# Pacing the loads of the first-layer weight pieces in SyncE's queue

## The chip, the core and the metric

The kernel runs on one core of one Trainium2 chip. A core has five engines that run side by side: TensorE (PE in the profile, its weight loads PEld), VectorE (DVE), ScalarE (ACT), GpSimd (POOL) and SyncE (SP). Here SyncE does nothing but issue DMA transfers, one after the other in the order of the program; ScalarE issues a few at the start and the end. The metric is the time of one execution on the device in microseconds (us). Three executions of the kernel before took 669.35, 664.38 and 667.37 us; the median is 667.37.

## The reference

Two blocks follow one another. The first is a delta-rule attention over 768 steps for 4 x 8 heads of size 48; the second is a layer pair with a learned negative slope on 3072 tokens.

```python
k_n = k / (np.linalg.norm(k, axis=-1, keepdims=True) + 1e-06)
for t in range(S):                                   # S = 768
    y[:, :, t] = np.einsum('bhd,bhde->bhe', q[:, :, t], state)
    v_old = np.einsum('bhde,bhd->bhe', state, kt)
    state = state + bt[:, :, :, None] * np.einsum('bhd,bhe->bhde', kt, vt - v_old)

x = y as (B*S, H*D) = (3072, 384)
h = x @ w_in                                         # (384, 2048)
g = np.maximum(h, 0.0) + alpha * np.minimum(h, 0.0)
out = g @ w_out                                      # (2048, 384)
```

`w_in` and `w_out` arrive as 8-byte floats; everything is computed in 4-byte floats.

## The kernel before, in words

The 768 steps are cut into 12 chunks of 64, and the 4 batches into 2 pairs, so that there are 24 attention steps `n`, each for one chunk and one pair. Inside a chunk the recurrence becomes small matrix products and the inverse of a triangular matrix, which VectorE makes by elimination for four steps at a time (`eliminate_small` for the first four, `eliminate` after that). When both pairs of a chunk are done, its 256 tokens go through the two layers. The order of every engine's instructions is written out by hand, and products of the layers are woven between those of the attention (`weave`, `alongside`).

**The weight pieces.** `w_in` is cut into 12 pieces of 128 rows by 512 columns; as 8-byte floats a piece is 512 KB. `weights` (L183) returns three things for such a list: `fetch` (L206) issues the loads on SyncE's queue, up to a given piece; `begin` (L220) has ScalarE turn the two 32-bit words of each number into parts of a 4-byte float (two instructions a piece, L226 and L227); `finish` (L232) has VectorE join them (L237, L242). A piece is first loaded into a stage, which is space that nothing else needs yet: pieces 0 to 5 lie in the later home of `w_out`, 6 and 7 in `space_out`, 8 and 9 in `more`, 10 in `sums`, and piece 11 again in the first stage. A second call of `weights` does the same for the 16 pieces of `w_out`.

**Where the loads stand in SyncE's queue.** Calls and lines are in this order: the first loads of `k`, `beta`, `q`, `v` (L137, L161, L174, L1584); `fetch_in(n_in)` and `fetch_in(n_in + 2)`, that is pieces 0 to 7 in a row (L1585, L1644, `n_in` is 6); `load_late(1)` and `load_v(2)`, that is four loads of `kl` and two of `v_raw` (L1646, L1647); three `load_early`, six loads of `ke` for steps 4, 5 and 6 (L1656); `fetch_in(n_in + 5)`, pieces 8 to 10 (L1657); `load_q(2)` and `load_q(3)`, four loads of `qp` (L1662); after the first chunk one `load_early` (L1525), `load_late(2)` (L1706), `fetch_in(n_in + 6)`, which is piece 11 (L1709), `load_late(3)` and `load_v(3)` (L1713, L1714), and so on.

**Who uses them.** ScalarE begins pieces 0 to 2 at L1671 and pieces 3 and 4 at L1674, right before it places the first inverses (`place_small`, L631, called from `first_chunk`); pieces 0 to 3 are joined inside `first_chunk`, the rest beside the second chunk (`second_pair`). The key blocks of steps 4, 5 and 6 are turned on TensorE in `first_chunk` (`flipped`, L404); the queries of steps 2 and 3 are turned at L1710 (`flips`, L404).

**Completion semaphores.** In the built program the DMA transfers take eight completion semaphores in turn, and a transfer is issued only when the one that used its semaphore before, eight transfers earlier, has landed.

Of the kernel before, what the change touches and what calls it, by code (L numbers as in the profile page):

```python
# [26 lines left out]
U32 = mybir.dt.uint32  # L27
# [16 lines left out]
def kernel(  # L44
# [11 lines left out]
    nc = tc.nc  # L56
# [13 lines left out]
    const = ctx.enter_context(tc.tile_pool(name="const", bufs=1))  # L70
# [109 lines left out]

    ahead = [0]

    def weights(pieces, stages, ids, done, limit=None, pool=False):  # L183

        count = len(pieces)
        fetched, begun = [], []

        def words(i):
            w = stages[ids[i]]
            dst, src = pieces[i]
            shape = list(dst.shape)
            n = shape[1] * (shape[2] if len(shape) > 2 else 1)  # L200
            w = w[:, 0 : 2 * n]
            if len(shape) > 2:
                return w.rearrange("p (f e) -> p f e", f=shape[1]), n
            return w, n

        def fetch(n):  # L206
            while len(fetched) < min(n, count):
                i = len(fetched)
                assert ids[i] not in ids[len(done) : i]
                nc.sync.dma_start(out=words(i)[0], in_=pieces[i][1].bitcast(U32))  # L210
                fetched.append(i)

        def flat(x):
            return x.rearrange("p f d -> p (f d)") if len(x.shape) > 2 else x

        def halves(i):
            w = flat(words(i)[0]).rearrange("p (e w) -> p e w", w=2)
            return w[:, :, 0], w[:, :, 1], flat(pieces[i][0])

        def begin(n):  # L220
            while len(begun) < min(n, count):
                i = len(begun)
                assert i < len(fetched)
                lo, hi, dst = halves(i)

                nc.scalar.activation(dst.bitcast(U32), lo, ACT.Copy, scale=2.0**-29)  # L226
                nc.scalar.activation(  # L227
                    lo.bitcast(FP32), hi.bitcast(FP32), ACT.Prelu, scale=2.0**-112, alpha=-(2.0**32)
                )
                begun.append(i)  # L230

        def finish():  # L232
            for i in range(count):
                begin(min(i + 2, max(ahead[0], i + 1)))
                lo, _, dst = halves(i)
                engine = nc.gpsimd if pool else nc.vector
                engine.tensor_scalar(  # L237
                    out=lo, in0=lo, scalar1=3, scalar2=None, op0=ALU.logical_shift_left
                )
                yield  # L240

                engine.tensor_tensor(  # L242
                    out=dst.bitcast(U32), in0=lo, in1=dst.bitcast(U32), op=ALU.add
                )
                done.append(i)
                n = len(fetched)
                while n < min(count, limit or count) and ids[n] not in ids[i + 1 : n]:
                    n += 1
                    fetch(n)
                yield  # L250

        return fetch, begin, finish()


# [12 lines left out]
    for t in range(2):  # L267
# [5 lines left out]
        out=ones, in_=ones, compare_op=ALU.is_ge, fill=1.0, base=0,  # L273
# [7 lines left out]
    for t in range(2):  # L281
# [5 lines left out]
        out=first_of, in_=ident.rearrange("p (q u e) -> p u q e", u=2, e=HB // 2)[:, 0],  # L287
# [7 lines left out]
        out=below[:, 0:1], in0=below[:, 0:1], scalar1=-1.0, scalar2=1.0, op0=ALU.mult, op1=ALU.add  # L295
    )
    nc.gpsimd.tensor_tensor(
        out=below[:, 1:2], in0=which[:, 1:2], in1=below[:, 1:2], op=ALU.subtract
# [1045 lines left out]
    in_done, out_done = [], []  # L1344
# [185 lines left out]
    def statics(first, last):  # L1530
# [18 lines left out]
    pieces = [  # L1549
        (w_in[:, i, o : o + W_IN_P], moe_w_in[i * 128 : (i + 1) * 128, o : o + W_IN_P])  # L1550
        for o in range(0, DFF, W_IN_P)
        for i in range(KT)
    ]
    n = 2 * W_IN_P
    n_in = FT * DM // n
    stages = [space[:, i * n : (i + 1) * n] for i in range(n_in)]
    spare_words = space_out.rearrange("p s e -> p (s e)")
    stages += [spare_words[:, i * n : (i + 1) * n] for i in range(2)]
    words = more.rearrange("p i s e -> p (i s e)").bitcast(U32)
    stages += [words[:, i * n : (i + 1) * n] for i in range(2)]  # L1560
    stages += [sums.rearrange("p i s e -> p (i s e)").bitcast(U32)[:, 2 * n : 3 * n]]
    ids = [*range(n_in + 5), 0]
    fetch_in, begin_in, conv_in = weights(pieces, stages, ids, in_done, n_in + 5)
    PARTS_IN = 2 * len(pieces)

    pieces = [(w_out[:, f], moe_w_out[f * 128 : (f + 1) * 128]) for f in range(FT)]
    stages = [space_out[:, i] for i in range(SPACES)]
    for f in range(FT // 2, FT, 2):
        stages.append(w_out[:, f : f + 2].rearrange("p f d -> p (f d)").bitcast(U32))
    ids = [0, 1, 2, 3, 4, 5, 6, 0, 1, 2, 6, 0, 1, 2, 0, 1]  # L1570
    fetch_out, _, conv_out = weights(pieces, stages, ids, out_done)
    PARTS_OUT = 2 * len(pieces)

# [362 lines left out]
```

## Time and profile before

| | |
|---|---|
| median of three runs | 667.37 us (664.38 to 669.35) |
| the profiled execution | 668.62 us, its span 666.9 us |
| PE busy | 640.3 us (96% of the span) |
| DVE busy | 490.6 us (74%) |
| ACT busy | 266.4 us (40%) |
| POOL busy | 94.8 us (14%) |
| moved by DMA | 37.69 MB, mean 57 GB/s |
| mean granted TensorE clock | 0.984 |

The span runs from the first to the last instruction; the execution is 1.7 us longer. The page cuts the span into 40 slices of 16.7 us and gives each engine's busy share in tenths, so that one sees where an engine is full. The chain of work that ended last starts at the last instruction and goes back, at each step, to what released it. SyncE's instructions are DMA issues: their start and duration say how long the queue was held, and the time to landing runs from the start of the issue until the data has arrived.

### The profile page before, as it was taken

How to read it: one execution, taken by the hardware profiler on the slowest of the kernel's cores; microseconds unless marked ns; L12 is line 12 of the kernel's file. 1: busy time of each engine (PE TensorE's matmuls, PEld its weight loads, DVE VectorE, ACT ScalarE, POOL GpSimd, SP SyncE). 2: the span in 40 equal slices, each digit the busy share in tenths (PEclk: the TensorE clock that was granted, in tenths of full speed). 3: DMA queues.
4: the chain of work that ended last, by engine and by line, in shares of the span. 5: the costliest groups of instructions: out<-in, count | busy, mean ns of one | idle time of the engine just before them, and what ended most of it. 6: DMA issues, size and time to landing. Idle time of an engine off the chain costs nothing.

```text
span 666.9 us, 21587 instructions
## 1 busy us (share of the span) xinstructions
PE 640.3 (96%) x9279; PEld 567.4 (85%) x9279; DVE 490.6 (74%) x1175; ACT 266.4 (40%) x619; POOL 94.8 (14%) x210
## 2 busy tenths in 40 slices
PE   5778799999999999999999999999999999999997
PEld 4576687756688998998998998998999999999997
DVE  4846679996899869748959748859869658568283
ACT  5835656525455343334334333223234245042140
POOL 7000021101010100001000000000035034053260
PEclk9969999999999999999999999999999999999999
DMA  7965545401342032022022022022112210100000
GB/s 117 287 144 117 179 106 126 104 18 32 65 94 40 17 67 49 15 61 49 15 48 38 15 48 37 14 49 37 27 37 38 36 37 4 25 14 1 25 1 25
DMA packets 111152, 37.69 MB, mean 57 GB/s; under 512 B 104224, under 2 KB 107440, under 8 KB 111056
## 3 DMA queue, kind: packets, MB, share of 16 engines
q1 hardware_dynamic: 109184, 35.81, 24.1%
q8 instruction: 73, 1.20, 0.7%
q10 hardware_dynamic: 1872, 0.49, 0.4%
q14 instruction: 23, 0.19, 0.1%
HBM read 31.56 MB, written 4.72 MB: 54 GB/s over the span
## 4 chain that ended last, share of the span: by engine, by line
PE 83%; DVE 9%; ACT 3%; issue 2%; DMA 1%; SPq 1%; POOL 0%; DVEq 0%; POOLq 0%; ACTq 0%
PE p_ffn L991 21%; PE p_ffn L1056 17%; PE p_more L1308 8%; PE p_ffn L1034 5%; PE p_more L1224 4%; PE p_ffn L1214 3%; PE p_ffn L1308 3%; PE p_ffn L1219 2%; PE p_pair L673 2%; PE p_pair L404 2%; PE p_pair L733 2%; PE p_pair L849 2%; PE p_pair L456 2%; PE p_pair L776 2%; PE p_pair L836 2%
## 5 line engine op out<-in xcount | busy, mean ns | idle before, releaser
L991 PE MATMUL p_ffn<-xt,w_in 128*128 128x256 f32 x768 | 177.5, 384 | 3.0 <-ACT w_out L226 1.2
L991 PEld LDWEIGHTS p_ffn<-xt,w_in 128*128 128x128 f32 x768 | 142.6, 190 | 24.5 <-issue 2.2
L1001 ACT ACTIVATE act<-p_ffn 128x512 f32<-128x512 f32 x56 | 33.3, 595 | 80.8 <-PE p_ffn L991 80.5
L1003 DVE SCALAR_TENSOR_TENSOR act<-act,al_t,p_ffn 128x256 f32<-128x256 f32 x112 | 48.5, 474 | 22.7 <-ACT act L1001 22.6
L561 DVE TENSOR_TENSOR block<-block,prod 128x30 f32<-128x30 f32 (+9 forms) x150 | 49.8, 332 | 5.2
L1248 POOL TENSOR_TENSOR k_t<-k_t 128x128 f32<-128x128 f32 (+1 forms) x48 | 29.6, 616 | 166.4 <-ACT k_t L1243 163.9
L555 DVE TENSOR_TENSOR prod<-block 128x30 f32<-128x30 f32 (+9 forms) x150 | 48.9, 326 | 1.4
L1056 PE MATMUL p_ffn<-w_out,act 128*128 128x192 f32 x288 | 49.6, 328 | 0.0
L393 POOL TENSOR_TENSOR beta_t<-beta_t,rec 128x8 f32<-128x8 f32 x24 | 6.2, 258 | 299.5 <-DVE rec L387 287.7
L896 ACT COPY xt<-p_pair 128x384 f32<-128x384 f32 x22 | 10.4, 479 | 91.2 <-PE p_pair L888 77.4
L1056 PEld LDWEIGHTS p_ffn<-w_out,act 128*128 128x128 f32 x288 | 46.5, 190 | 0.3
L1248 POOL TENSOR_TENSOR block<-block 128x128 f32<-128x128 f32 (+1 forms) x48 | 28.0, 583 | 16.7 <-ACT block L1243 14.1
L1214 PE MATMUL p_ffn<-xt,w_in 128*128 128x256 f32 x96 | 28.7, 380 | 0.0
L743 DVE TENSOR_TENSOR r<-v_raw,p_pair 64x192 f32<-64x192 f32 (+1 forms) x66 | 23.3, 352 | 2.2 <-PE p_pair L733 1.2
L685 ACT COPY inv<-p_pair 32x256 f32<-32x256 f32 x40 | 14.5, 361 | 24.9 <-DVE u L840 24.2
L725 ACT COPY y<-p_pair 128x384 f32<-128x384 f32 x22 | 10.4, 480 | 32.3 <-PE p_pair L721 30.7
L1076 DVE TENSOR_TENSOR o_sb<-u,p_ffn 128x192 f32<-128x192 f32 x24 | 8.0, 352 | 20.4 <-PE p_ffn L1056 20.0
L1262 DVE SCALAR_TENSOR_TENSOR act<-block,al_t,act 128x256 f32<-128x256 f32 x32 | 19.1, 638 | 5.1 <-ACT block L1258 5.1
L1308 PE MATMUL p_more<-w_out,act 128*128 128x192 f32 x128 | 21.9, 329 | 0.0
L1243 ACT COPY k_t<-p_more 128x512 f32<-128x512 f32 x16 | 9.4, 586 | 30.6 <-PE p_more L1224 25.9
L1034 PE MATMUL p_ffn<-w_out,act 128*128 128x384 f32 x64 | 21.5, 489 | 0.0
L733 PE MATMUL p_pair<-beside,k_t 48*64 48x112 f32 x704 | 21.3, 259 | 0.2 <-ACT beside L432 0.2
(275 smaller groups left out, 1408.2 us busy)
## 6 DMA issues: line engine op xcount, KB each, us to landing
qp<-in_q_dram SPq DMA_DIRECT2D x48, 96.0 KB, 3.0
v_raw<-in_v_dram SPq DMA_DIRECT2D x48, 96.0 KB, 2.9
kl<-in_k_dram SPq DMA_DIRECT2D x96, 48.0 KB, 2.6
out_dram<-o_sb SPq DMA_DIRECT2D x90, 48.0 KB, 1.6
space_out<-in_moe_w_out_dram SPq DMA_DIRECT2D x11, 384.0 KB, 3.5
ke<-in_k_dram SPq DMA_DIRECT2D x43, 96.0 KB, 3.1
w_out<-in_moe_w_in_dram SPq DMA_DIRECT2D x7, 512.0 KB, 5.8
w_out<-in_moe_w_out_dram SPq DMA_DIRECT2D x5, 384.0 KB, 7.0
```

Source lines behind the costliest of these rows:

```text
L555: nc.vector.tensor_tensor(out=prod, in0=r[:, 0:j, j : j + 1].to_broadcast([128, j, n]), in1=r[:, j : j + 1, j + 1 : HB].to_broadcast([128, ...
L561: nc.vector.tensor_tensor(out=r[:, 0:j, j + 1 : HB], in0=r[:, 0:j, j + 1 : HB], in1=prod, op=ALU.add)
L733: nc.tensor.matmul(p[half(t ^ a), a, g], k_t[n][dims(a), g, half(t)], beside[bp][dims(a), t, g])
L991: nc.tensor.matmul(p_h[:, i], w_in[:, t, (f + i) * 128 : (f + i + 1) * 128], xt[:, t], start=(t == 0), stop=(t == KT - 1),)
L1001: nc.scalar.activation(g, p_h, ACT.Relu, scale=-1.0)
L1003: nc.vector.scalar_tensor_tensor(out=g[:, i], in0=g[:, i], scalar=al_t[:, f + i : f + i + 1], in1=p_h[:, i], op0=ALU.mult, op1=ALU.add,)
L1034: nc.tensor.matmul(p_o[u], gs[f // 2][:, f % 2, u * 128 : (u + 1) * 128], w_out[:, f], start=(f == 0), stop=(f == FT - 1),)
L1056: nc.tensor.matmul(p, x(i), w(i), start=(i == 0), stop=(i == FP - 1))
L1214: nc.tensor.matmul(p[:, f * 256 : f * 256 + 256], w(2, f), xt[:, 2], start=True, stop=False)
L1224: nc.tensor.matmul(q[:, j], a, b, start=True, stop=True)
L1248: nc.gpsimd.tensor_tensor(out=dst, in0=a, in1=b, op=ALU.add)
L1308: nc.tensor.matmul(p, x(i), w(i), start=(i == 0), stop=(i == FP - 1))
```

## The change

`weights` takes a further argument `apart`, which only the call for `w_in` sets, to 2. Before piece `i` is issued, `paced` puts a DMA copy of 4 bytes into SyncE's queue: it reads one word of the stage of piece `i - 2` (for piece 11, of piece 10) and writes it to a new small tile `held_back`, which nothing reads. As the copy reads what the earlier piece's load writes, SyncE waits for that landing before it issues the copy, and what stands behind it in the queue waits too. Pieces 0 and 1 have no such copy; pieces 2 to 11 do, so ten copies are added. In the built program all other instructions of SyncE and those of the other engines keep their order.

```diff
+    holds, held_back = [], const.tile([1, 16], U32, name="held_back")
+
-    def weights(pieces, stages, ids, done, limit=None, pool=False):
+    def weights(pieces, stages, ids, done, limit=None, pool=False, apart=None):
...
+        def paced(i, apart):
+
+            if i >= apart:
+                before = words(i - apart)[0]
+                before = before if len(before.shape) == 2 else before[:, 0]
+                nc.sync.dma_start(out=held_back[0:1, len(holds) : len(holds) + 1], in_=before[0:1, 1:2])
+                holds.append(i)
+
         def fetch(n):
             while len(fetched) < min(n, count):
                 i = len(fetched)
                 assert ids[i] not in ids[len(done) : i]
+                if apart:
+                    paced(i, apart if i < 11 else 1)
                 nc.sync.dma_start(out=words(i)[0], in_=pieces[i][1].bitcast(U32))
                 fetched.append(i)
...
-    fetch_in, begin_in, conv_in = weights(pieces, stages, ids, in_done, n_in + 5)
+    fetch_in, begin_in, conv_in = weights(pieces, stages, ids, in_done, n_in + 5, False, 2)
```

## The prediction

> **What bounds the kernel now.** I read the page's slices and its chain first, then the chain from 27 to 64 us, then SyncE's and ScalarE's timelines there, and last the DMA issues piece by piece.
>
> ```profile
> PE   5778799999999999999999999999999999999997
> ...
> PE 83%; DVE 9%; ACT 3%; issue 2%; DMA 1%; SPq 1%; POOL 0%; DVEq 0%; POOLq 0%; ACTq 0%
> ```
>
> From the seventh slice (100 us) on, TensorE is full; there the change moves nothing. All pieces are loaded in the first 60 us, where TensorE is 50 to 80% busy and the chain goes from engine to engine. A microsecond won or lost there goes through to the end, unless it falls into a wait that something else sets. The chain there:
>
> ```profile
> 29.58 0.36 DVE inv L627
> 29.94 0.14 issue
> 30.07 2.45 PE p_pair L776 x103
> 32.52 1.37 issue
> 33.89 2.62 PE p_pair L776 x70
> ...
> 55.60 0.60 SPq L161
> ...
> 58.32 0.60 SPq L137
> 58.92 0.05 issue
> 58.97 3.65 DMA v_raw<-in_v_dram
> ```
>
> Two places matter: the inverse at 29 to 37 us, beside which ScalarE converts pieces, and 50 to 62 us, where SyncE's queue itself is on the chain: loads stand one behind the other until `v_raw` of step 3 lands, for which VectorE sat idle 4.42 us.
>
> SyncE's queue around the pieces (start, us, issues):
>
> ```profile
> 15.39 3.28 SPq L210 DMA_DIRECT2D w_out<-in_moe_w_in_dram  x6
> 18.79 0.90 SPq L210 DMA_DIRECT2D space_out<-in_moe_w_in_dram  x2
> 19.79 4.21 SPq L161 DMA_DIRECT2D kl<-in_k_dram  x4
> 24.89 1.87 SPq L137 DMA_DIRECT2D v_raw<-in_v_dram  x2
> 27.99 7.00 SPq L137 DMA_DIRECT2D ke<-in_k_dram  x6
> 35.03 2.09 SPq L210 DMA_DIRECT2D more<-in_moe_w_in_dram  x2
> ```
>
> Eight pieces leave in 4.3 us and then drain: from 18 to 27 us the DMA moved 399 GB/s, one piece per 1.3 us. Asked for single issues, the DMA view gives for piece 0 and piece 4:
>
> ```profile
> w_out<-in_moe_w_in_dram SPq DMA_DIRECT2D x1, 512.0 KB, 4.2
> w_out<-in_moe_w_in_dram SPq DMA_DIRECT2D x1, 512.0 KB, 7.3
> ```
>
> So 4.2 us with nothing large ahead, and more with each piece ahead (piece 1: 4.9). Pieces 0 and 1 land at 19.5 and 20.8 us, piece 4 at 24.9, piece 7 at 30.3.
>
> **The change, part by part.** *The copies' own cost.* The trace has no 4-byte copy. The nearest rows of SyncE are a piece's issue, 0.43 us, and the issue of a small table (`al_sb`, 8 KB), 0.60 us. I take 0.45 with the 0.05 us between issues, so 0.5 a copy (bounds 0.4 and 0.65). Nobody waits for a copy to land.
>
> *Pieces 2 to 7.* Each round of two is one landing (4.2 us) plus a copy's issue (0.5): 4.7 us where before a round took 2.6. Piece 2 is issued at 20.0 and lands at 24.2; piece 4 lands at 19.5 + 2 x 4.7 = 28.9; piece 6 at 33.6, piece 7 at 20.8 + 3 x 4.7 = 34.9 (issued at 30.6). ScalarE asks for piece 2 at 24.75, piece 3 at 26.62 (lands at 25.5) and piece 4 at 27.90:
>
> ```profile
> 27.90 0.68 ACT L226 ACTIVATE w_in<-w_out 128x512 uint32<-128x512 uint32 x1
> 28.62 0.68 ACT L227 ACTIVATE w_out<-w_out 128x512 f32<-128x512 f32 x1
> 29.31 0.91 ACT L631 ACTIVATE inv<-inverse,which 128x256 f32<-128x256 f32 x2
> 31.38 0.59 ACT L795 COPY act<-p_pair 128x512 f32<-128x512 f32 x1 [1.16 <-PE p_pair L776]
> ```
>
> Only piece 4 is late, by 1.0 us. Behind it on ScalarE wait the inverse of step 1 (L631), which TensorE needs at 31.87, and the copy L795, before which ScalarE sat idle 1.16 us. So up to 1.16 us costs nothing; I take 0. With piece 1's 4.9 us and 0.65 a copy, piece 4 lands at 30.6, 2.7 late, and costs 1.6. Earlier than now it can't bring anything: ScalarE waited for no piece there.
>
> *What queues behind piece 7.* Four `kl` and two `v_raw` start at 31.1 instead of 19.8, at 0.65 us each; the keys of step 4 are issued at 35.0 and 35.7 and land by 39.9 (4.2 us is the slowest of the six `ke` landings now, 3.1 the quickest). TensorE turns them at 40.86: covered, by 1 us. One of these six issues held the queue for 2.01 us instead of 0.63; one such stall ahead would make it 0.4 us late. Steps 5 and 6 are turned at 47.18 and 49.36, far later. `kl` and `v_raw` of this group are used at 52.47 and 57.73.
>
> *Pieces 8 to 10 and the queries.* The six `ke` end at 39.0, pieces 8 and 9 with their copies at 40.9. The copy for piece 10 waits for piece 8: issued at 39.5, landing 5.3 us later as now, at 44.8. Piece 10 leaves at 45.3, then four `qp` until 48.4 instead of 40.9. They land in 5.4 to 7.0 us now, behind three pieces, so the first two by 52 behind one; they are turned at 53.09. SyncE is next needed at 50.38, which leaves 2 us. ScalarE begins pieces 8 to 10 at 60.95 or later. Cost 0.
>
> *Piece 11.* Its copy (piece 10 landed long before) stands between `load_late(2)` and piece 11, in the stretch where the queue is on the chain. Behind it wait piece 11, four `kl` and the two `v_raw`. This 0.5 us nothing hides: `v_raw` lands that much later, and VectorE and TensorE behind it (TensorE idle for 2.23 us until 65.51).
>
> *Sum.* 0.5 (bounds 0.4 and 0.65) + 0 (to 1.6) + 0 (to 0.4) = +0.5 us, upper bound 2.65. The profiled execution of 668.62 would take 669.1; it lies 1.25 above the median of the runs, so against the median I forecast **667.9**. The runs shown spread by 5 us, and 1% (6.7 us) is about what a measurement of this kernel can tell from no change.
>
> The Trainium skill, "DMA: Bandwidth & Descriptors", section "Anatomy of one DMA", gives about 2.0 us fixed plus bytes by 436 GB/s, fitted for GpSimd's path; as an estimate that is 3.2 us for a piece, against 4.2 in this trace. By it a round would take 3.7 us, piece 4 would land at 26.9, and the sum would stay at +0.5. The rule speaks against pacing all the same: two pieces in flight leave the fixed part uncovered.
>
> **Rivals.** *1. Two in flight land as slowly as five did (slower).* Place: ScalarE's wait for piece 4. It decides from a landing of 4.3 us on (19.5 + 2 x 4.8 = 29.1, where the 1.16 us are used up), and each further microsecond costs two. At piece 4's present 7.3 us: 19.5 + 2 x 7.8 = 35.1, 7.2 late, less 1.16, plus 0.5: +6.5, and 674. For it: the threshold is near, and small `k` packets share the queue. Against it: landings grew with the number ahead, and here at most one is ahead. At 4.9 us a piece and 0.65 a copy the price is 2.2, 669.6.
>
> *2. TensorE's stalls without a wait go (faster).* Between 15 and 70 us two "issue" gaps of 1.37 and 1.50 us stand before L776; the instruction queue fetched 16 KB during each (start 31.16 and 41.64), and one took 1.37 us, another 0.88. Fewer pieces in flight could serve them sooner. At most 2.87 - 0.5 = 2.4 us less: 665.0. Against it: after each fetch 1.4 to 1.5 us passed before TensorE went on, and pieces are in flight at both times after the change too. The Trainium skill, "DMA: Bandwidth & Descriptors", section "Queues, rings and completion order", says that each DMA engine turns between queues packet by packet; by that rule the weights never held a fetch long, and the sum stays at +0.5.
>
> *3. The granted clock falls elsewhere.* Windows (length, PE busy and count, PEld, DVE, ACT, POOL, clock, DMA):
>
> ```profile
> 32.00:37.00 5.00, 3.11 (x103) 2.76 (x96) 1.16 (x2) 1.17 (x2) 0.00 (x0) 0.50 0.51 95
> 37.00:47.50 10.50, 8.20 (x262) 7.51 (x263) 5.24 (x11) 3.65 (x8) 0.00 (x0) 0.66 0.75 191
> 47.50:53.00 5.50, 5.50 (x82) 4.68 (x80) 4.23 (x12) 3.81 (x8) 0.00 (x0) 0.64 0.12 22
> 53.00:60.00 7.00, 6.88 (x162) 5.91 (x155) 4.58 (x10) 4.01 (x8) 0.00 (x0) 1.00 0.69 151
> ```
>
> The clock drops to 0.50 after TensorE's idle 2.5 us at 27.5. If idle times move and it stays up from 37 to 53, the 13.7 us of matmuls shrink by up to 4.8, with rival 2 to 660.2; if it drops from 53 to 60, up to 6.9 are added, to 674.8. The Trainium skill, "TensorE: Matmul & The Clock Gate", Part 1, says that activity is judged in free-running windows of 3.4 us; by that, which way it goes is chance from run to run.
>
> *4. The change doesn't pace.* If the copies don't hold the pieces, only their issues stay: piece 7 and what follows 3 us later with ample cover, and 0.5 at piece 11: 667.9 again.
>
> **From this to the numbers.** Forecast 0.54. Rival 1: 0.16, half of it near 670 and half beyond 1%. Rival 2: 0.12. Rival 3: 0.14, of it 0.05 slower by over 1%, 0.06 faster by over 1%, 0.03 within. Rival 4: 0.04. Faster by over 1% is then 0.06 and a rounding, 0.07; slower 0.08 + 0.05 = 0.13; within 0.80. The range leaves out rival 1's far half and rival 3's ends (0.19): from 665.0 less 1 to 670 plus 2 for the spread of the medians, 664 to 672.
>
> **What would show it.** Right: SyncE's issues of pieces 2 to 7 in pairs some 4.7 us apart, landings near 4.2 us, GB/s from 18 to 32 us nearer 225 than 399; ScalarE idle about 1 us before piece 4 (now L239), L795 still released by TensorE; turning the keys of step 4 not waiting for a DMA; about 0.5 us more before `v_raw` of step 3. Wrong: landings of 5 us and more with an idle ScalarE ahead of L631's successor, a DMA as releaser of L404, the two "issue" gaps gone, or half clock in other stretches.

## The result and the profile after

| | before | after |
|---|---|---|
| median of nine runs each, same chip | 667.73 us (664.38 to 669.36) | 671.47 us (669.59 to 672.08) |
| profiled execution | 668.62 us | 670.56 us |
| its span | 666.9 us | 668.8 us |
| mean granted TensorE clock | 0.984 | 0.987 |

The ratio is 1.0052, with a 95% interval from 1.0032 to 1.0071: the changed kernel takes about 3.5 us longer (2.1 to 4.7). That lies within 1%, the forecast's likeliest case, and inside its range, but it is clear of zero, and the sum in the prediction was 0.5 us.

The page of the changed kernel first: the row of TensorE and of its clock in 40 slices, and the shares of the chain.

```profile
PE   5777799999999999999999999999999999999997
...
PEclk9978799999999999999999999999999999999999
...
PE 80%; DVE 12%; DMA 2%; issue 2%; ACT 2%; SPq 1%; POOL 0%; DVEq 0%; POOLq 0%
```

The row of TensorE differs from the one before in the fourth slice alone (7 for 8, 50 to 67 us), and from the sixth slice on it is full again. What TensorE lost on the chain (83% to 80%) went to VectorE (9% to 12%) and to waits for DMA (1% to 2%). So the place to look at is the one the prediction named, the first 60 us. SyncE's queue in the changed kernel there (start, us, issues):

```profile
20.06 0.62 SPq L214 DMA_DIRECT2D held_back<-w_out  x1
20.72 0.38 SPq L223 DMA_DIRECT2D w_out<-in_moe_w_in_dram  x1
23.52 0.58 SPq L214 DMA_DIRECT2D held_back<-w_out  x1
24.15 0.38 SPq L223 DMA_DIRECT2D w_out<-in_moe_w_in_dram  x1
...
30.32 0.38 SPq L223 DMA_DIRECT2D space_out<-in_moe_w_in_dram  x1
30.81 2.72 SPq L161 DMA_DIRECT2D kl<-in_k_dram  x4
33.57 2.38 SPq L137 DMA_DIRECT2D v_raw<-in_v_dram  x2
36.00 4.84 SPq L137 DMA_DIRECT2D ke<-in_k_dram  x6
...
45.81 0.58 SPq L214 DMA_DIRECT2D held_back<-more  x1
46.44 0.38 SPq L223 DMA_DIRECT2D sums<-in_moe_w_in_dram  x1
46.92 2.77 SPq L137 DMA_DIRECT2D qp<-in_q_dram  x4
49.80 1.55 SPq L137 DMA_DIRECT2D ke<-in_k_dram  x2
51.45 3.57 SPq L161 DMA_DIRECT2D kl<-in_k_dram  x4
55.06 0.64 SPq L214 DMA_DIRECT2D held_back<-sums  x1
55.80 0.34 SPq L223 DMA_DIRECT2D w_out<-in_moe_w_in_dram  x1
56.67 2.70 SPq L161 DMA_DIRECT2D kl<-in_k_dram  x4
59.46 1.27 SPq L137 DMA_DIRECT2D v_raw<-in_v_dram  x2
```

The copies hold the queue (L214, each 0.57 to 0.73 us), pieces 2 to 7 leave in pairs, and everything behind moves: the queries leave from 46.92 on instead of 37.70. At 49.80 the loads for step 7 (`ke`, one call of `load_early`) follow with no pause; before, the queue stood idle from 40.9 until 50.38 at this place:

```profile
37.70 3.21 SPq L137 DMA_DIRECT2D qp<-in_q_dram  x4
50.38 1.75 SPq L137 DMA_DIRECT2D ke<-in_k_dram  x2
```

The last line of the changed kernel's queue is the issue of `v_raw` of step 3, 59.46 instead of 58.32.

TensorE's longest waits from 15 to 70 us in the changed kernel (waits by what ended them: total, times, longest):

```profile
PE p_pair L789 <- issue: 4.4, 2, 4.0
PE p_pair L417 <- DVE w_out L250: 1.6, 1, 1.6
...
PE p_pair L417 <- DMA qp<-in_q_dram: 1.1, 1, 1.1
```

Two of these are new: TensorE now waits for queries before it turns them (L417; the wait of 1.6 us put down to VectorE ends as the last query lands, at 54.46). The first line was 2.9, 2, 1.5 before. The chain shows the same two places:

```profile
30.49 1.81 PE p_pair L789 x104
32.31 3.98 issue
36.28 1.62 PE p_pair L789 x79
...
40.03 0.40 issue
...
47.66 4.59 DMA qp<-in_q_dram
...
52.38 0.64 PE p_pair L417 x4
...
60.11 3.58 DMA v_raw<-in_v_dram
```

The stall without a wait behind the first inverse is 3.98 us for 1.37, the second 0.40 for 1.50. The queries' load, which was on no chain before, is on it, and behind it come loads again, up to `v_raw` of step 3. VectorE takes that at 63.78 instead of 62.71 us.

From there to the end it takes 605.1 us after and 604.2 before; so of the 1.9 us between these two executions 1.1 arise ahead of this moment and 0.9 behind it. In all 14 profiles of this study (before, after and the twelve experiments) this rest lies between 604.2 and 605.1 us, while the moment itself lies anywhere from 60.3 to 66.4. Most of the difference between kernels is made ahead of it.

### The profile page after: what moved, and what is told of

It is laid out like the page before. It is cut to its first block, busy times and chain, and to the rows that moved or that the text cites. A ratio compares the mean times of both kernels' runs of the same rounds, so it can differ in the third digit from the quotient of the medians.

```text
span 668.8 us, 21603 instructions
## 1 busy us (share of the span) xinstructions
PE 640.3 (96%) x9279; PEld 565.9 (85%) x9279; DVE 491.5 (73%) x1175; ACT 266.1 (40%) x619; POOL 94.2 (14%) x210
## 4 chain that ended last, share of the span: by engine, by line
PE 80%; DVE 12%; DMA 2%; issue 2%; ACT 2%; SPq 1%; POOL 0%; DVEq 0%; POOLq 0%
PE p_ffn L1004 19%; PE p_ffn L1069 17%; PE p_more L1321 8%; PE p_ffn L1047 5%; PE p_more L1237 4%; PE p_ffn L1227 3%; PE p_ffn L1321 3%; PE p_ffn L1232 2%; PE p_pair L789 2%; PE p_pair L417 2%; PE p_pair L862 2%; PE p_pair L686 2%; PE p_pair L746 2%; PE p_pair L469 2%; PE p_pair L849 2%
## 5 line engine op out<-in xcount | busy, mean ns | idle before, releaser
L574 DVE TENSOR_TENSOR block<-block,prod 128x30 f32<-128x30 f32 (+9 forms) x150 | 49.9, 332 | 5.1
L568 DVE TENSOR_TENSOR prod<-block 128x30 f32<-128x30 f32 (+9 forms) x150 | 48.9, 326 | 1.4
L1089 DVE TENSOR_TENSOR o_sb<-u,p_ffn 128x192 f32<-128x192 f32 x24 | 8.0, 352 | 20.5 <-PE p_ffn L1069 20.0
L1256 ACT COPY k_t<-p_more 128x512 f32<-128x512 f32 x16 | 9.4, 586 | 30.6 <-PE p_more L1237 25.9
```

The source lines that it names most:

```text
L568: nc.vector.tensor_tensor(out=prod, in0=r[:, 0:j, j : j + 1].to_broadcast([128, j, n]), in1=r[:, j : j + 1, j + 1 : HB].to_broadcast([128, ...
L574: nc.vector.tensor_tensor(out=r[:, 0:j, j + 1 : HB], in0=r[:, 0:j, j + 1 : HB], in1=prod, op=ALU.add)
```

## The experiments

The experiments were timed in three series (e1 to e4, e5 to e9, e10 to e13), each on a chip of its own; a ratio is always to the kernel before on that same chip. Three theories run through the expectations. **F**: TensorE's stall (the gap at L776, L789 in the changed kernel, right behind the first inverse) grows since the fetch of its code comes late while pieces are in flight. **Q**: SyncE's queue is through with pieces and queries too late, and so is what stands behind them. **C**: the copy at piece 11, on the chain, is the cost.

| run | what is paced or moved | ratio to before | 95% interval | first stall (us) | TensorE ready for the queries (us) | `v_raw` of step 3 issued (us) | VectorE takes it (us) |
|---|---|---|---|---|---|---|---|
| before |  | 1 |  | 1.37 | 53.09 | 58.32 | 62.71 |
| after | all | 1.0052 | 1.0032 to 1.0071 | 3.98 | 51.25 | 59.46 | 63.78 |
| e5_after_again | all | 1.0053 | 1.0033 to 1.0072 | 4.18 | 52.18 | 60.56 | 64.42 |
| e7_two_to_ten | all but piece 11 | 1.0051 | 1.0031 to 1.0071 | 3.13 | 51.68 | 62.02 | 66.34 |
| e6_queries_ahead | all, queries first | 1.0043 | 1.0025 to 1.0061 | 2.32 | 50.26 | 62.52 | 66.43 |
| e12_paced_order_changed | all, 6 to 10 behind queries | 1.0054 | 1.0030 to 1.0078 | 2.88 | 49.89 | 60.25 | 64.57 |
| e1_first_eight | 2 to 7 | 1.0021 | 1.0006 to 1.0035 | 2.04 | 53.31 | 59.76 | 64.53 |
| e4_copies_of_ident | copies, no pacing | 1.0016 | 0.9990 to 1.0041 | 2.09 | 52.75 | 59.36 | 63.18 |
| e3_eleven_only | 11 | 1.0020 | 1.0004 to 1.0035 | 1.76 | 52.05 | 58.56 | 62.98 |
| e2_eight_to_ten | 8 to 10 | 0.9976 | 0.9956 to 0.9996 | none | 51.32 | 56.38 | 60.35 |
| e13_eight_to_ten_again | 8 to 10 | 0.9989 | 0.9969 to 1.0009 | none | 50.48 | 56.27 | 60.30 |
| e9_six_to_ten_late | nothing; 6 to 10 behind queries | 1.0009 | 0.9994 to 1.0023 | 2.02 | 50.32 | 56.44 | 61.06 |
| e10_queue_held | nothing; 14 copies ahead of 8 | 1.0009 | 0.9990 to 1.0028 | none | 47.68 | 57.16 | 61.49 |
| e11_in_flight | nothing; 8 and 9 earlier | 1.0008 | 0.9988 to 1.0027 | none | 50.90 | 56.75 | 60.91 |

Ratios are over many executions, the last four columns from the one that was profiled of each kernel; so a column orders the runs, it does not add up to a ratio. "None" means that the gap right behind the inverse is absent; later gaps at the same line are there in those four runs.

### The parts by themselves

Four runs cut the change into parts; each edit is against the changed kernel. Pieces 2 to 7 alone:

```diff
-                if apart:
-                    paced(i, apart if i < 11 else 1)
+                if apart and i < 8:
+                    paced(i, apart)
```

> Only pieces 2 to 7 are paced; 8 to 11 go as before. Theory F (the code stall): pieces 6 and 7 are still moving when TensorE asks for code at 30 us, its first stall grows from 1.37 to about 4 us as in the changed kernel, and this run keeps most of the loss: 2 to 3 us slower than before. Theory Q (late queries): the copy for piece 10 no longer waits for piece 8, so the four qp are issued some 4 us earlier than in the changed kernel (from about 42.5) and land by about 50, before TensorE turns them: at most 1 us slower than before. Theory C (the issue of the copy at piece 11, 0.6 us): nothing from it here.

Measured: 1.0021, or 1.4 us (0.4 to 2.3), between what F and Q asked for. Pieces 8 to 10 alone, in two series:

```diff
+                if apart and 8 <= i < 11:
+                    paced(i, apart)
```

> Only pieces 8, 9 and 10 are paced. F: pieces 6 and 7 have landed by 30.3 as before, the first stall stays at 1.4 us: no loss. Q: piece 8 lands at about 40.3, piece 10 is issued at about 41, the qp from 41.5 to 44.2, and they land by about 49, before 53: no loss either, since the queue was not held before. C: nothing. All within 1 us of before.

> The run with only pieces 8 to 10 paced, once more: it came out 0.24% faster than before with an interval that ended 0.04% below one, which no theory here asks for. If it is real, it comes out between 0.995 and 0.999 again; if it was chance, at one.

Measured: 0.9976 and 0.9989, the second interval with no difference inside. SyncE's queue in the second of them:

```profile
40.93 2.76 SPq L137 DMA_DIRECT2D qp<-in_q_dram  x4
...
48.35 1.68 SPq L137 DMA_DIRECT2D ke<-in_k_dram  x2
...
56.27 1.65 SPq L137 DMA_DIRECT2D v_raw<-in_v_dram  x2
```

The queries are through at 43.7 us, with 4.6 us to spare before step 7's keys. That those keys are already asked for at 48.35, and not at 50.38 as in the profile of before, shows that this moment is not fixed. The first stall is absent in this execution, yet TensorE did not go without: two gaps of 0.84 and 2.72 us stand at L789 a little later, 3.6 us in all, and before had 2.9.

```profile
PE p_pair L789 <- issue: 3.6, 2, 2.7
```

Piece 11 alone, and the copies without the pacing:

```diff
+                if apart and i == 11:
+                    paced(i, 1)
```

> One copy only, ahead of piece 11. C: it takes 0.6 us of SyncE's queue where the queue is on the chain, v_raw of step 3 lands 0.6 us later, and the time is 0.6 us longer (0.1%). F and Q: nothing.

```diff
-                before = words(i - apart)[0]
-                before = before if len(before.shape) == 2 else before[:, 0]
-                nc.sync.dma_start(out=held_back[0:1, len(holds) : len(holds) + 1], in_=before[0:1, 1:2])
+                nc.sync.dma_start(out=held_back[0:1, len(holds) : len(holds) + 1], in_=ident[0:1, 1:2].bitcast(U32))
```

> All ten copies stay, but read a word of the identity matrix, which is there from the start; so they take SyncE's queue and the completion semaphores, and hold no piece for the landing of the one two ahead (through the eight semaphores a piece still waits for the one four ahead). F: pieces 2 to 7 leave earlier than in the changed kernel, piece 7 by about 23 us and landed by 31 as before: first stall near 1.4 us, so about 1 us slower than before at most. Q: the six ke end at about 38 instead of 41, the qp by about 45: no wait for them. C: 0.6 us. Together about 0.6 us slower than before.

Measured: 1.0020 and 1.0016, the first just clear of no difference, the second not. In the profile of e3_eleven_only `v_raw` of step 3 left only 0.24 us later than before.

What follows: pieces 2 to 7 (+0.21%) and 8 to 10 (-0.24% and -0.11%) add up to no loss, or a few hundredths of a per cent. The whole change costs 0.52%. Most of the loss comes only when parts are together.

### Both together, without piece 11

> The changed kernel once more, unchanged, as the anchor for the runs beside it and for a second profile. All theories: 0.5% slower than before, 3 to 4 us. F: the code fetch at the inverse starts about 3 us after TensorE begins to use the inverse (33.6 us), not about 1.2 us after it as before. Q: TensorE waits at the second chunk's queries for 1 to 2.5 us.

The changed kernel, measured once more in the same series: 1.0053. In this second profile TensorE waited 1.7 us for the queries. And the kernel without the copy at piece 11:

```diff
-                if apart:
-                    paced(i, apart if i < 11 else 1)
+                if apart and i < 11:
+                    paced(i, apart)
```

> The changed kernel without the copy ahead of piece 11. C: 0.6 us less than the changed kernel by the issue's length, 1.3 us less by what the run with that copy alone measured; so about 2.5 us slower than before. Q and F: the loss of the changed kernel stays but for that.

Measured: 1.0051, the same loss. C falls as the main cause: without its copy nothing is won back. Pieces 2 to 7 and 8 to 10 cost 0.51% together and about nothing when added up from the runs above; as an estimate from the intervals, the gap is 0.4 to 0.5%, give or take 0.3. The chain of e7_two_to_ten says how they meet:

```profile
43.67 5.72 DMA more<-in_moe_w_in_dram
...
49.41 0.58 SPq L214
...
50.03 0.38 SPq L223
...
51.25 5.13 DMA qp<-in_q_dram
...
56.52 1.07 PE p_pair L417 x4
...
58.73 2.66 PE p_ffn L1004 x8
61.39 0.54 SPq L161
...
62.02 0.59 SPq L137
...
62.67 3.58 DMA v_raw<-in_v_dram
```

Read downwards: piece 8 lands, only then the copy for piece 10 (L214) leaves the queue, then piece 10 (L223), then the queries, and TensorE waits for them. The chain then goes on through the turning of the queries and the first products of a layer to the loads of `kl` and `v_raw`, whose issues wait for TensorE. So here the new wait of the change is on the path, from beginning to end. The execution that was profiled took 673.07 us, above its kernel's median of 671.72. The wait is there because pieces 2 to 7 had put piece 8 late (its issue at 43.67; 35.03 before): one part takes the spare time in the queue, the other part then overruns it.

### The queue held by something else, and pieces in flight

The kernel before, with 14 copies of a constant ahead of piece 8, which hold the queue and pace nothing (`hold` issues them, its definition is left out here):

```diff
+    hold(14)
     fetch_in(n_in + 5)
```

> The kernel before, nothing paced, with 14 copies of one word of the identity matrix ahead of piece 8 (0.64 us each, 9 us in all): the queue alone is late, as in the changed kernel from piece 8 on, and pieces 0 to 7 are as before. Q (the lateness of SyncE's queue sets the end of the head: the qp end near 50 us, and load_early, load_late and v_raw of step 3 behind them are issued 1 to 2 us late): 1.5 to 3 us slower than before. F (the code fetch is late because pieces 6 and 7 are in flight when the inverse is used): fetch as before at about 31.3 us, stall about 1.4 us, no loss.

Measured: 1.0009, no difference shown. Queue and wait in its profile:

```profile
43.82 2.90 SPq L137 DMA_DIRECT2D qp<-in_q_dram  x4
46.83 3.64 SPq L137 DMA_DIRECT2D ke<-in_k_dram  x2
```

```profile
PE p_pair L410 <- DMA qp<-in_q_dram: 3.9, 1, 3.9
```

The queue was through at 46.7 and not, as was meant, at 50: the six `ke` (5.27 us for 7.00), the copies (8.41 for 9) and pieces 8 and 9 (0.87 for 2.09) all held it less. TensorE waited for the queries here too, 3.9 us, but its stalls at this line (L782 here) were 1.1 us in all and it was early, ready at 47.68; `v_raw` of step 3 left at 57.16. This run holds the queue by less than the changed kernel does and so doesn't test the lateness of 50 us and more.

The kernel before, with pieces 8 and 9 already ahead of the `ke` loads:

```diff
+    fetch_in(n_in + 4)
     for n in range(1, NJ):
```

> The kernel before, nothing paced and no copy, with pieces 8 and 9 issued ahead of the six ke instead of behind them: two pieces leave at about 28 and 30 us as pieces 6 and 7 do in the changed kernel, and the queue carries the same work as before, so the qp end near 41. F: the fetch starts at 33 us or later, TensorE's stall is 3 us or more instead of 1.4, and the time is 1 to 2.5 us longer. Q: no change, within 0.5 us.

Measured: 1.0008. In this execution the 16 KB fetch on the instruction queue came at 23.4 us, before those pieces left at 27.3. So the run tells nothing on F.

### The order changed

Pieces 8 to 10 behind the queries, in the changed kernel:

```diff
-    fetch_in(n_in + 5)
...
         load_q(i + 2)
+    fetch_in(n_in + 5)
```

> The changed kernel with pieces 8 to 10, copies and all, issued behind the four qp instead of ahead of them. Q: the qp are issued from about 41 to 44 and land by 48, TensorE doesn't wait for them, and 1.5 to 2.5 us of the loss go: 1.5 to 2 us slower than before. F: pieces 6 and 7 are as in the changed kernel, the stall stays near 4 us, and the loss stays at 3 us or more.

Measured: 1.0043, still a loss, and the interval overlaps that of the changed kernel widely. The first stall was 2.32 us and not near 4, as F asked. The profiled execution again lies above its kernel's median (672.75 us to 670.89). Queue, and VectorE's longest wait from 55 to 72 us:

```profile
43.53 2.65 SPq L137 DMA_DIRECT2D qp<-in_q_dram  x4
...
52.08 2.16 SPq L137 DMA_DIRECT2D ke<-in_k_dram  x2
...
62.52 1.70 SPq L137 DMA_DIRECT2D v_raw<-in_v_dram  x2
```

```profile
DVE v_raw L723 <- DMA v_raw<-in_v_dram: 10.2, 1, 10.2
```

The queries came early, and the lateness went to the next in the queue: step 7's keys leave at 52.08, `v_raw` of step 3 at 62.52, and VectorE sat 10.2 us for it. The wait has to stand somewhere ahead of these loads, and there is not enough room for it.

Last, pieces 6 and 7 moved behind the queries as well, once without pacing and once with it:

```diff
-    fetch_in(n_in + 2)
...
-    fetch_in(n_in + 5)
...
         load_q(i + 2)
+    fetch_in(n_in + 5)
```

> The kernel before, nothing paced and no copy, but pieces 6 to 10 issued in one row behind the four qp. F: pieces 0 to 5 have landed by 26.2 us; the small key and value loads end sooner, and the pieces 6 to 10 then move from about 30 to 38 us, right when TensorE asks for code: the fetch at the inverse starts 2 us later than before and the time is 1 to 3 us longer. Q: the qp land 8 us earlier than before, where nobody waited for them: no change. If only the number of pieces ahead of the inverse mattered, it would be faster.

> The changed kernel with all its copies, but pieces 6 to 10 issued behind the kl, v_raw, ke and qp loads instead of among them: no piece is in flight from 30 to 33 us, the qp are issued by about 36, and SyncE is through with piece 10 at about 47. F and Q both take their cause away here: 0.5 to 1 us slower than before for the copy at piece 11 and not 3.5. If the loss were in the pacing of pieces 2 to 5 or in the copies as such, it would stay at 3 us.

Measured: 1.0009 without, 1.0054 with. The order by itself costs nothing that shows, where F asked for 1 to 3 us; the pacing keeps its whole price, where 0.5 to 1 us was expected. The paced run's queue:

```profile
49.73 0.39 SPq L223 DMA_DIRECT2D sums<-in_moe_w_in_dram  x1
50.23 1.40 SPq L137 DMA_DIRECT2D ke<-in_k_dram  x2
...
55.88 0.64 SPq L214 DMA_DIRECT2D held_back<-sums  x1
...
60.25 2.12 SPq L137 DMA_DIRECT2D v_raw<-in_v_dram  x2
```

It is again through with the pieces only at 50.1 us, and the copy for piece 11 now really waits: piece 10, issued at 49.73, landed at 55.80, and the copy left at 55.88. The stall at L789 was 2.88 us here although pieces 6 and 7 were not in flight at that time; F, in the form that was tested (those two pieces delay the fetch), is not borne out.

### What the runs say together

All five runs with both parts paced (four kernels, one measured twice) lose 0.43 to 0.54%; in their profiles the queue is through with queries and pieces 8 to 10 between 49.7 and 54.0 us, and `v_raw` of step 3 leaves at 59.46 or later. In the nine others (before among them) the queue is through by 47.3 us, and none loses more than 0.21%; `v_raw` leaves by 58.56 in seven of them, and at 59.36 and 59.76 in e4_copies_of_ident and e1_first_eight. Q is what the runs agree with, and in e7_two_to_ten the chain shows it from end to end. In e6_queries_ahead waits for TensorE of 0.3 to 0.6 us among the last loads come on top of the late queue.

Did TensorE itself come late, held up by its stalls? By the table, no. It stands ready for the queries at 49.9 to 52.2 us in the five profiles that lose, and at 47.7 to 53.3 in the nine others; the means are 51.1 and 51.3. VectorE takes `v_raw` at 63.8 to 66.4 us against 60.3 to 64.5, means 65.1 and 61.9. So 3.2 us of the 3.5 by which these profiled executions differ on average arise between the two moments, where loads of SyncE's queue are waited for. In the changed kernel's chain the first stall does stand ahead of the queries' load, since the second `qp` issue waited for TensorE (L862); but that wait was 0.4 us. All this rests on one profile for each run, and no run held the queue past 47.3 us without both parts paced; so it is strong support for Q, and not a test by an edit of its own.

In the profile of the changed kernel itself 1.1 us arise ahead of `v_raw`, of which 0.96 stem from the place of piece 11 (from its copy's start to the next `kl` issue 1.61 us pass; from piece 11's issue to that `kl`, 0.65 before). Not all of this is the copy: a pause of 0.45 us behind piece 11, for which the profile names nothing, is in it, and e7_two_to_ten and e10_queue_held, which have no copy there, take 1.06 and 1.08 us from piece 11 to that `kl`.

Whether pacing lengthens the first stall stays open. It is 2.0 to 4.2 us in the six profiles with the first pieces paced (2 to 7, or 2 to 5 in e12_paced_order_changed), 1.4 to 2.1 in four of the unpaced, and absent in the other four. Where it is absent, a 16 KB fetch on the instruction queue lies at 23 to 24 us, and the stalls come later. None of the six paced profiles had that, four of eight others had. But all stalls at that line together are 2.0 to 4.4 us in the six and 1.1 to 5.6 in the eight, so the loss doesn't follow them.

No version was clearly quicker than the kernel before: pacing 8 to 10 alone gave 0.9976 and then 0.9989.

## Why the prediction was right or wrong

**The copies' own cost**: mis-sized a little. They held the queue 0.57 to 0.73 us, not 0.45; with the pause behind one 0.61 to 0.79, above the upper bound of 0.65 in five of the ten.

**Pieces 2 to 7**: right. Piece 7 left at 30.32 (30.6 forecast). Pieces landed with a median of 4.2 us, over the eleven whose landing the trace has (4.7 in the second profile of the same kernel), and 18 to 32 us moved 220 GB/s, for 225 forecast and 399 before. Piece 7 alone took 6.8 us, which nobody waited for. ScalarE in the changed kernel:

```profile
28.25 0.69 ACT L239 ACTIVATE w_in<-w_out 128x512 uint32<-128x512 uint32 x1 [0.59 <-DMA w_out<-in_moe_w_in_dram]
...
31.71 0.58 ACT L808 COPY act<-p_pair 128x512 f32<-128x512 f32 x1 [1.07 <-PE p_pair L789]
```

It waited 0.59 us for piece 4, which landed at 28.23, and L808 is still released by TensorE after 1.07 us of idle time: the cover held, cost 0 in this profile. **Rival 1** needed landings above 4.3 us for pieces 2 to 4 and did not happen (4.0, 4.2 and 4.1). The estimate of 3.2 us a piece from the Trainium skill ("DMA: Bandwidth & Descriptors", "Anatomy of one DMA"), whose figures are for GpSimd's path, stays too short for this queue. That few loads in flight leave its fixed part uncovered fits the halved GB/s; no run takes it apart.

**What queues behind piece 7**: right in its outcome, off in a size. TensorE did not wait for step 4's keys at 42.98 (the second load landed at 40.82). But the six `ke` ended at 40.84, not 39.0: where the prediction allowed for one long issue, three came (0.97, 1.01 and, in a `v_raw` ahead of them, 1.70 us).

**Pieces 8 to 10 and the queries**: this step failed. "SyncE is next needed at 50.38, which leaves 2 us … Cost 0." Its parts were each 1 to 2 us out, all to the same side: the six `ke` ended 1.8 us late, piece 10 left at 46.44 for 45.3, the queries were through at 49.7 for 48.4. And the date they were held against moved the other way: TensorE was ready for the queries at 51.25, not 53.09, and waited 1.1 and 1.6 us. In five of the eight other profiles whose queue was through by 47.3 us, step 7's keys were asked for between 46.8 and 48.9 us. The prediction took 50.38 from one execution, in which TensorE had run at half clock for 17.0 us ahead of its queries (31.0 to 41.2 and 44.7 to 51.5; 6.8 us after) and had stood for 2.87 us in stalls; it was a late date, not a due time. Against dates of 46.8 to 48.9, a queue through at 49.7 to 54.0 has no slack left. It is this step with no cost and no upper bound above zero that should have carried microseconds.

**Piece 11**: the place was right, the size was not. Where the queue is on the chain the stretch took 0.96 us longer in the changed kernel's profile, not 0.5; the copy put piece 11's issue off by 0.74, from 55.06 to 55.80. By itself it measured +0.20% (0.04 to 0.35), in the profile 0.24 us, since before piece 11 waited there for VectorE's join in any case. Without it, the change loses as much.

**Rival 2** was half right: the two "issue" gaps do change, but the first went from 1.37 to 3.98 us and the second from 1.50 to 0.40, 1.5 us more in sum and not 2.4 less. Even so TensorE was ready for the queries 1.84 us earlier than before, so the gaps did not make it late. The prediction read the fetches as lying in the gaps; before, they ended at 32.53 and 42.52, where the gaps begin. In all 14 profiles TensorE went on from such a gap 1.2 to 1.7 us after a 16 KB fetch on the instruction queue had ended (in the changed kernel the fetch ran from 33.57 us on, for 1.32 us). The Trainium skill ("Runtime: NRT & Kernel Launch", "Instruction fetch mechanics") calls the cost of crossing such a block mostly hidden; at this place, with 104 matmuls in 1.81 us, a gap of 3.98 us stood around the fetch.

**Rival 3**: half-clock stretches moved (before 31.0 to 41.2, 44.7 to 51.5 and 65.1 to 68.5 us; after 37.5 to 44.3, 54.6 to 58.0 and 75.1 to 81.9), yet there are 17.1 us of them for 20.5, and the mean clock is 0.987 for 0.984. The clock is not where the time went.

**Rival 4**: excluded; the pairs in the queue show the pacing.

So the forecast within 1% held by its spread and its cases, not by its sum: 0.5 us was added for piece 11, and some 3 us came that the sum had at nothing, from two parts of the change that cost about nothing when each is made alone.

## What to carry to other kernels

A wait in an in-order queue delays everything behind it, so pacing transfers there is to be counted down to the last load that some engine needs soon; moving one of these ahead only passes the lateness to the next. Slack read from one execution is slack against that execution's own delays: hold a new wait against the earliest moment at which the work could be due, and add the delays of several edits ahead of the same date before calling any of them covered. Two edits that cost nothing alone can use up the same spare time, which only a run with both shows.

## What was not expected of the hardware

A copy of 4 bytes held SyncE's queue longer, 0.57 to 0.73 us, than the load of a 512 KB piece, 0.34 to 0.43 us in the changed kernel.

The first 16 KB fetch on the instruction queue after 20 us came at 23 to 24 us in four profiles and at 31 to 34 in ten, and the gaps at L776 or L789 added up to between 1.1 and 5.6 us. That spread is as large as the effect under study, and a reason to read no difference of a few microseconds from two single profiles.

A piece of 512 KB with at most one other ahead took 3.7 to 4.9 us to land in the changed kernel (median 4.2), but 6.8 us once, for piece 7, with small `kl` and `v_raw` loads issued behind it.
